# Last projection in 96-column tiles, quartered K tiles in layer 1, one contiguous output DMA: a decode kernel on one core

## The chip, the cores and the metric

The kernel runs on one core of a Trainium2 chip. The metric is the device time of one execution in microseconds (us). Three runs of the kernel before gave 2551.93, 2552.01 and 2552.08 us; their median is 2552.01 us.

## The reference

Two token rows (B = 2, one token each, D = 576 columns) go through two layers. A layer has two blocks, each with its input normalised and added back to the residual x. Cut to what matters:

```python
x = x + A(layernorm(x), k_cache, v_cache, wq, wo)    # 32 heads of 128, 16384 cached positions
x = x + B(layernorm(x), w1, w2, w3, w4)

# A: q = x @ wq; softmax(q . K / sqrt(128)) @ V, per batch row and head; then @ wo
# B: h = gelu(layernorm(x) @ w1), shifted along the sequence, @ w2 -> hs
#    x1 = x + hs
#    return x1 + gelu(layernorm(x1) @ w3) @ w4      # w3: 576x4608, w4: 4608x576
```

The output is x after both layers, 2 x 576 in bf16. The K and V caches are 64 tiles of 4 MiB each (two rows by 32 heads), and both layers read all of them.

## The kernel before, in words

**Layout.** x is held transposed: 128 partitions by KT = 5 column tiles by B = 2. Four tiles cover columns 0 to 511, the fifth covers columns 448 to 575, and only its upper 64 partitions count (`kcol`, `TL` = 64). A projection with few output columns (`rows_step`, line 908 for its matmuls) loads a 128 x 128 block of the weight matrix into TensorE as the stationary operand and streams two columns of activations through it, so that each matmul has two moving columns and one weight load of 128 columns. For w4 these are 36 blocks of K times 5 column tiles, 180 matmuls.

**Memory and queue.** Weights and caches go through one SBUF area, `mem`, with six slots of 32 KiB per partition (`plan_all`, `Store`). Every load is issued by SyncE (line 98) in the order in which `plan_all` queues it. `Store.pump` issues the next load of the queue as soon as the cells it needs have been released, and it waits for the readers of those cells. A whole K or V tile is 128 rows of 32 KiB; a tile planned in `parts` is loaded in that many pieces, each with its own wait.

**Attention.** For each of the 64 (row, head) pairs, half of the scores come from TensorE (transposes at line 1184, evacuation by ScalarE at line 1200, matmuls at 1210) and half from VectorE (`dots`, multiply at line 1240, sum at 1244). `used` releases a whole tile in halves. The pairs run in a loop made by `Graph.loop`.

**Between the layers.** Three K tiles and two V tiles of layer 0 are kept for layer 1. The first K tile of layer 1 is transposed while layer 0 ends: `ahead` issues a group of eight transposes (line 1184), `lay` the ScalarE copy back into the tile (line 699); both do nothing in the tail of layer 1. There are 14 such groups and two more that are held over. They are placed by hand: in `attention`, `last_head`, `two_norms`, the w3 projection, `groups_projection` (w4), `input_norm` and the wq projection of layer 1. In layer 1 `early_scores` (line 1225) reads that tile, and the loads of the first new tiles wait for it and for its followers: V of pair 61 in 4 parts, K of pair 0 whole, K of pair 1 in 2 parts.

**The tail of layer 1.** After the last pair come wo (five loads), `two_norms`, w3 (`cols_projection`, lines 835 and 845), the gelu (lines 995 to 1000), then w4 in eight groups of 6, 6, 6, 6, 6, 3, 2 and 1 blocks (`groups_projection`). Between groups stand a norm on the side (`side_norm`, with a stationary operand in float32, line 711) and the small w1 projection (`h_projection`, line 1337). w1 is loaded by `plan_small`: four full row blocks in one DMA, then the last 64 rows in two DMAs of 56 and 8 rows. Two VectorE additions (`add_rows`, line 596) make `xo`; `finish` transposes its five tiles back on TensorE (line 1316), copies 2 x 576 out of PSUM (line 1319), and SyncE writes the two rows to DRAM.

Of the kernel before, what the change touches and what calls it, by code (L numbers as in the profile page):

```python
# [32 lines left out]
class Graph:  # L33
# [48 lines left out]
        o.deps += [w for w in dict.fromkeys(self.writer[k] for k in reads)]  # L82
        return o

    def dma(self, sem, starts, reads=(), writes=()):

        if sem not in self.dma_sems:
            self.dma_sems[sem] = self.nc.alloc_semaphore(sem)
            self.dma_count[sem] = 0
        o = Op("sync", None)  # L90
        o.sem = sem
        self.dma_count[sem] += 16 * len(starts)
        o.val = self.dma_count[sem]
        h = self.dma_sems[sem]

        def fn(sp):
            for dst, src in starts:
                sp.dma_start(dst, src).then_inc(h, 16)  # L98
            return None
        o.fn = fn  # L100
        return self._add(o, reads, writes)
# [230 lines left out]
class KB:  # L332
    NL = 2
# [13 lines left out]
    PK = ["prod", "gT", "hf", "every", "y0", "y"]  # L347
    GROUPS = (6, 6, 6, 6, 6, 3, 2, 1)
    HEAD = (200, 60)

    def __init__(self, nc, A_x, K, V, wq, wo, w1, w2, w3, w4, out):
        self.nc = nc
# [30 lines left out]
    def _alloc(self):  # L383
        nc = self.nc
        sb = nc.alloc_sbuf_tensor
        B, U, KT, MT, NL = self.B, self.U, self.KT, self.MT, self.NL
        self.size = self.AUX + self.NSLOT * self.TILE
        self.mem = sb("mem", [128, self.size // 2], BF16)
        w = self.CH * 128
# [47 lines left out]
        self.junk = sb("junk", [128, 1], FP32)  # L437
        self.xn2 = sb("xn2", [128, NL, KT, B], BF16)
        self.zero = sb("zero", [128, KT, B], BF16)
        self.xo = sb("xo", [128, KT, B], BF16)  # L440
        self.mv = sb("mv", [128, 3, B], FP32)
        self.hm = sb("hm", [128, 2, B], FP32)
        self.sc = sb("sc", [128, 9, B], FP32)
# [65 lines left out]
    def plan_all(self):  # L509

        B, D = self.B, self.D
        row, w3r, wqr = 2 * D, 2 * self.F, 2 * 128 * self.H
        g = [row * n for n in self.GROUPS]
        self.cuts, self.korder = {}, {}
        s = [self.slot(i) for i in range(self.NSLOT)]
        source = {"k": self.K, "v": self.V}

        tiles = self.tile_order(0)
        place = [(i + 2) % 6 for i in range(len(tiles))]
        place[-1] = 4  # L520
# [14 lines left out]
        b = a + w3r // 2  # L535
        c = b + 4 * g[0]
        e = b + g[6] + g[7]
        self.plan_groups(0, [b, b + g[0], b + 2 * g[0], b + 3 * g[0], 0, g[4], b, b + g[6]])
        assert c <= s[1] and g[4] + g[5] <= b and e <= c
        self.plan_cols("wq", 1, self.wq, [full(1, hd, e), full(2, hd, e + wqr), full(3, hd, e + 2 * wqr),  # L540
                                          full(4, hd, 0), full(0, hd, wqr // 2)])
        assert e + 3 * wqr <= s[1] and wqr // 2 + wqr <= e

        tiles = self.tile_order(1)
        ring = [i if i < 2 else (i + 1) % 6 for i in range(len(tiles))]
        for i, (t, u) in enumerate(tiles):
            self.plan_tile(source[t], t, u, ring[i], (4, 1, 2)[i] if i < 3 else 1, None if i else [1, 2, 3, 0])
        assert ring[-6:] == [4, 5, 0, 1, 2, 3]
        self.plan_heads(1, [s[4], s[4] + r8, s[4] + 2 * r8, s[5], s[4] + 3 * r8])
        a = s[5] + row * self.WO_CUT  # L550
        self.plan_small("w1", 1, self.w1, a, (0, 56, 64))
        a += row * self.KT
        self.plan_cols("w3", 1, self.w3, [full(0, mt, a), full(1, mt, a + w3r), full(2, mt, s[0]), full(3, mt, s[0] + w3r),
                                          full(4, mt, s[0] + 2 * w3r)])
        assert a + 2 * w3r <= self.size
        b = s[0] + 2 * w3r + w3r // 2
        assert b + g[0] <= s[1]
        self.plan_groups(1, [b, s[1], s[1] + g[1], s[1] + g[1] + g[2], s[1] + 3 * g[1], s[1] + 4 * g[1], s[2], s[2] + g[6]])
# [50 lines left out]
    def build(self):  # L609
# [11 lines left out]
                  reads=["ident"], writes=["ident"])  # L621
        for t, k in ((self.x, "x"), (self.st[:, 1, :, :], "st1"), (self.st[:, 2, :, :], "st2"), (self.xb[:, :, :], "xb"),
                     (self.x1[:, :, :], "x1"), (self.hs[:, :, :], "hs"), (self.zero[:, :, :], "zero"),
                     (self.xn[:, :, :], "xn"), (self.xo[:, :, :], "xo"), (self.xn2[:, :, :, :], "xn2"),
                     (self.q_f[:, :], "q_f")):
            self.pool(lambda e, t=t: e.memset(t, 0.0), writes=[k])
        def f(e):
# [31 lines left out]
    def layer(self, l):  # L659
# [6 lines left out]
        self.spread_tail()  # L666
        z = self.sps[0][:, 0:self.MT * self.B]
        self.cols_projection("w3", l, z, ("sps", 0), self.MT)
        self.between_norms()
        self.gelu_z(z)  # L670
        self.groups_projection(l)

# [64 lines left out]
    def input_norm(self, l):  # L737
        self.tt(self.st[:, 1, :, :], self.x, self.x, ALU.mult, ["x"], ["st1"])
        self.stats(2, self.mps, "mps", self.flat(0, 2), ["x", "st1"])
        self.ahead(1 - l, 2)  # L740
        self.scale_of()
        self.touch(ACT.Exp)
        self.lay(1 - l, 2)
# [3 lines left out]
    def two_norms(self, l):  # L747
# [2 lines left out]
        self.tt(self.st[:, 1, :, :], self.x, self.x, ALU.mult, ["x"], ["st1"])  # L750
        self.tt(self.st[:, 2, :, :], self.x, self.hs[:, :, :], ALU.mult, ["x", "hs"], ["st2"])
        self.stats(3, self.mps, "mps", self.flat(0, 3), ["x", "st1", "st2"])
        self.ahead(l, 3)
        m, e2, xc, y0, y = self.mv[:, 0, :], self.mv[:, 1, :], self.kb(self.xc), self.kb(self.y0), self.kb(self.y)
        self.tt(s[:, 0, :], m, m, ALU.mult, ["mv"], ["s0"])
        self.tt(s[:, 5, :], m, hm[:, 0, :], ALU.mult, ["mv", "hm"], ["s5"])
# [10 lines left out]
        self.recip(s[:, 6, :], s[:, 4, :], ["s4"], ["s6"])  # L767
        self.sqrt(s[:, 7, :], s[:, 6, :], ["s6"], ["s7"])
        self.touch(ACT.Sigmoid)
        self.lay(l, 4)  # L770
        self.tt(self.xn[:, :, :], y, self.over_k(s[:, 7, :]), ALU.mult, ["y", "s7"], ["xn"])

    def between_norms(self):

        KT, TL = self.KT, self.TL
        n, y0 = KT - 1, self.kb(self.y0)
# [2 lines left out]
        self.dv(lambda e: e.tensor_copy(out=self.xb[:, 0:n, :], in_=y0[:, 0:n, :]), reads=["y0"], writes=["xb"])  # L779
        self.dv(lambda e: e.tensor_copy(out=self.xb[TL:, n, :], in_=y0[TL:, n, :]), reads=["y0"], writes=["xb"])  # L780
        self.tt(self.x, self.x, self.x1[:, :, :], ALU.add, ["x", "x1"], ["x"])

    def side_norm(self, l):

# [112 lines left out]
                 ["mv", "hm"], ["hm"])  # L897
        self.tt(self.hsc[:, :, :], self.hs[:, :, :], self.over_k(self.hm[:, 0, :]), ALU.subtract, ["hs", "hm"], ["hsc"])

    def rows_step(self, buf, a, b, ps, rhs, rk, pk, nm, first):  # L900

        KT, B, D = self.KT, self.B, self.D

        def f(pe):
            for k in range(a, b):
                for t in range(KT):
                    o = (k - a) * D + self.kcol[t]
                    ins = pe.matmul(ps[:, t * B:(t + 1) * B], lhsT=buf[:, o:o + 128], rhs=rhs(k),
                                    start=first and k == a and t == 0, stop=False, skip_group_check=True)
            return ins  # L910
        self.pe(f, reads=[rk] + self.store.keys(nm), writes=[pk])
# [65 lines left out]
    def groups_projection(self, l):  # L977
        n = len(self.GROUPS)
        for i, (a, b) in enumerate(self.cuts["w4", l]):
            nm = ("w4", l, i)  # L980
            self.rows_step(self.store.buf(nm), a, b, self.mps, lambda k: self.gT[:, k * self.B:(k + 1) * self.B],
                           "gT", "mps", nm, i == 0)
            if i < 3:
                self.ahead(l, 1)
            if i < 4:
                self.lay(l, 1)
            if i == 1:
                self.side_norm(l)
            if i == 2 and l == self.NL - 1:
                self.h_projection()  # L990
        last = l == self.NL - 1
        self.add_rows(self.xo[:, :, :] if last else self.x, "xo" if last else "x", self.mps, "mps")

    def gelu(self, z, zk, a, b, dst, keys):
        self.act(lambda e: e.activation(out=a, in_=z, func=ACT.Square), reads=[zk], writes=keys)
# [86 lines left out]
    def last_head(self, l, s, u):  # L1082
# [11 lines left out]
        self.normed(l, 0, first)  # L1094
        self.ahead(l, 1)
        self.dealt(0, late, self.sps[2], ("sps", 2), self.masked[0], self.oA[:, :], "oA")
        self.ahead(l, 1)
        self.softmax_exp(s)
        self.touch(ACT.Sqrt)
        self.lay(l, 2)  # L1100
# [59 lines left out]
    def used(self, l, t, u, b0, n):  # L1160
# [1 line left out]
        if l == 0 and (t, u) in self.held():  # L1162
            return
        whole = (t, u) in self.store.where
        parts = 2 if whole else self.parts[t, u]
        size = self.NB // parts
        part = b0 // size
        self.uses[t, u, part] = self.uses.get((t, u, part), 0) + n
        if self.uses[t, u, part] == size:
            del self.uses[t, u, part]  # L1170
            if whole:
                self.store.release((t, u), part * self.TILE // 2, (part + 1) * self.TILE // 2)
            else:
                self.store.release((t, u, part))

# [133 lines left out]
    def finish(self):  # L1309
        g, KT, B, D = self.g, self.KT, self.B, self.D  # L1310
        mb = self.mps[:, :].bitcast(BF16)

        def f(pe):
            for t in [KT - 1] + list(range(KT - 1)):
                c = self.kcol[t]
                ins = pe.transpose(mb[0:B, c:c + 128], self.xo[:, t, :], self.ident[:, :])
            return ins
        self.pe(f, reads=["xo", "ident"], writes=["mps"])
        self.dv(lambda e: e.tensor_copy(out=self.rows[0:B, 0:D], in_=mb[0:B, 0:D]), reads=["mps"], writes=["prod"])
        o = g.dma("out", [(self.out.rearrange("b s d -> (b s) d"), self.rows[0:B, 0:D])], reads=["prod"])  # L1320
        g.op("sync", lambda sp: None, reads=["out_done"])
        g.ops["sync"][-1].deps.append(o)

# [66 lines left out]
```

## Time and profile before

| what | value |
|---|---|
| median of three runs | 2552.01 us |
| the profiled execution, its own time | 2552.28 us |
| span of its profile | 2550.6 us |
| read from HBM | 1094.21 MB |
| mean rate over the span | 429 GB/s |
| busy: PE, DVE, ACT, POOL | 60%, 74%, 44%, 6% |

The span runs from the first to the last instruction of the profile; 1.68 us of the profiled execution lie outside it. PE is the row of the matmuls, PEld that of the weight loads, which overlap the matmuls. A line such as L908 is line 908 of the kernel; a helper such as the SyncE issue (L98) has one line for all its calls. In the timeline a row begins with its start and its busy time in us, then engine, line, operation and operands, a count, and in brackets the idle time before it and what ended it.

### The profile page before, as it was taken

The numbers are of one execution on the slowest core, as the hardware profiler recorded it, in microseconds if no ns is written. First come the engines' busy times: TensorE is split into PE (matmuls) and PEld (weight loads), VectorE is DVE, ScalarE is ACT, GpSimd is POOL, SyncE is SP. The second block draws the span as 40 slices with busy tenths as digits, with TensorE's granted clock in tenths as the row PEclk, the third lists the DMA queues.
The fourth block names the chain that finished last, engine by engine and source line by source line (L and its number), as shares of the span: only waits on it lengthen the run. The fifth ranks groups of instructions, "written<-read, shape, count | busy, mean of one in ns | idle before, by whom it ended". The sixth has DMA issues, their size and how long they took to land.

```text
span 2550.6 us, 75213 instructions
## 1 busy us (share of the span) xinstructions
PE 1522.6 (60%) x34456; PEld 1432.9 (56%) x34456; DVE 1888.3 (74%) x1924; ACT 1113.7 (44%) x1831; POOL 162.1 (6%) x151
## 2 busy tenths in 40 slices
PE   4655555655555565556687655655565565556556
PEld 4555555555555555555677655555555455555555
DVE  5877777777777777777649877777777777777773
ACT  3434443443444344444355544443444344344432
POOL 0000000000000000000000000000000000000000
PEclk8666666666666666666667666666666666666665
DMA  9999999999999999999999999999999999999999
GB/s 412 428 434 430 433 431 433 430 433 431 433 431 433 430 433 430 433 430 434 425 417 431 431 434 430 433 430 433 430 433 430 434 430 433 431 433 431 433 431 376
DMA packets 44900, 1094.77 MB, mean 429 GB/s; under 512 B 4922, under 2 KB 6334, under 8 KB 9662
## 3 DMA queue, kind: packets, MB, share of 16 engines
q1 hardware_dynamic: 44862, 1094.23, 100.0%
q8 instruction: 28, 0.46, 0.1%
q14 instruction: 10, 0.08, 0.0%
HBM read 1094.21 MB, written 0.00 MB: 429 GB/s over the span
## 4 chain that ended last, share of the span: by engine, by line
DMA 71%; DVE 19%; issue 8%; PE 1%; SPq 0%; POOLq 0%; DVEq 0%; ACT 0%
DMA mem<-in_A_k_cache_dram 64%; DVE s_dve L1244 9%; DVE prod L1240 9%; DMA mem<-in_A_wo_dram 3%; DMA mem<-in_B_w_dram 2%; DMA mem<-in_A_v_cache_dram 2%; DMA mem<-in_A_wq_dram 0%; DVE mx L1249 0%; PE tps L1184 0%; DVE diag L1138 0%; DVE mx L1257 0%; SPq L98 0%; DVE q_col L1129 0%; DVE o_acc L1281 0%; DVE mx L1255 0%
## 5 line engine op out<-in xcount | busy, mean ns | idle before, releaser
L1200 ACT ACTIVATE mem<-tps 128x1024 bf16<-128x1024 bf16 x1018 | 955.7, 1036 | 1290.0 <-PE tps L1184 1287.5
L1184 PE MATMUL tps<-ident,mem 128*128 128x128 bf16 x8256 | 823.3, 271 | 707.8 <-POOLq L187 707.2
L1244 DVE TENSOR_REDUCE s_dve<-prod 128x16 f32<-128x2048 bf16 x508 | 1161.3, 2286 | 17.4
L1184 PEld LDWEIGHTS tps<-ident,mem 128*128 128x128 bf16 x8256 | 677.6, 124 | 717.7 <-POOLq L187 716.8
L1240 DVE TENSOR_TENSOR prod<-mem,qb 128x2048 bf16<-128x2048 bf16 x508 | 620.6, 1222 | 527.4 <-POOLq L187 518.9
L1300 PE MATMUL mps<-p,mem 128*128 128x1 bf16 x16384 | 450.7, 165 | 85.3 <-POOLq L187 78.2
L1300 PEld LDWEIGHTS mps<-p,mem 128*128 128x128 bf16 x16384 | 443.3, 103 | 100.2 <-ACT p L1274 97.0
L1210 PE MATMUL sps<-q_col,mem 128*128 128x1 bf16 x8144 | 368.7, 167 | 159.2 <-ACT mem L1200 142.9
L1210 PEld LDWEIGHTS sps<-q_col,mem 128*128 128x128 bf16 x8144 | 320.3, 101 | 217.4 <-ACT mem L1200 212.7
L1260 POOL PARTITION_ALL_REDUCE mx<-mx x128 | 160.2, 1252 | 2331.1 <-DVE mx L1257 2331.1
L1270 ACT ACTIVATE p<-s_dve,mx 128x64 bf16<-128x64 f32 x128 | 44.5, 348 | 15.5
L1148 ACT ACTIVATE qb<-sps 128x128 bf16<-128x128 f32 x129 | 34.0, 263 | 33.5 <-PE sps L1145 33.5
L1145 PE MATMUL sps<-diag,ones_bf 128*128 128x128 bf16 x129 | 29.8, 231 | 21.6 <-DVE diag L1138 21.6
L1274 ACT ACTIVATE p<-sps,mx 128x64 bf16<-128x64 f32 x128 | 37.5, 293 | 0.0
L1268 ACT ACTIVATE mx<-mx 128x1 f32<-128x1 f32 x128 | 30.6, 239 | 14.4 <-POOL mx L1260 14.4
L1138 DVE TENSOR_SCALAR diag<-ident,q_f 128x128 bf16<-128x128 bf16 x129 | 31.6, 245 | 0.0
L1249 DVE TENSOR_REDUCE mx<-s_dve 128x1 f32<-128x64 f32 x128 | 28.2, 220 | 4.5
L835 PE MATMUL sps<-xn,mem 128*128 128x2 bf16 x544 | 21.8, 175 | 12.3 <-DMA mem<-in_A_wq_dram 6.2
L835 PEld LDWEIGHTS sps<-xn,mem 128*128 128x128 bf16 x544 | 20.7, 122 | 13.5 <-DMA mem<-in_A_wq_dram 6.8
L1255 DVE TENSOR_REDUCE mx<-sps 128x1 f32<-128x64 f32 x128 | 27.4, 214 | 0.7 <-DVEq L259 0.7
L1145 PEld LDWEIGHTS sps<-diag,ones_bf 128*128 128x128 bf16 x129 | 12.6, 97 | 22.6 <-DVE diag L1138 22.6
L1274 ACT ACTIVATION_READ_ACCUMULATOR p<-sps,mx (+1 forms) x128 | 24.2, 189 | 0.0
(115 smaller groups left out, 225.8 us busy)
## 6 DMA issues: line engine op xcount, KB each, us to landing
mem<-in_A_v_cache_dram SPq DMA_DIRECT2D x125, 4096.0 KB, 45.5
mem<-in_A_k_cache_dram SPq DMA_DIRECT2D x124, 4096.0 KB, 43.1
mem<-in_B_w_dram SPq DMA_DIRECT2D x10, 864.0 KB, 15.0
mem<-in_A_wq_dram SPq DMA_DIRECT2D x8, 1024.0 KB, 12.5
mem<-in_A_wo_dram SPq DMA_DIRECT2D x6, 1152.0 KB, 38.6
mem<-in_B_w_dram SPq DMA_DIRECT2D x6, 1152.0 KB, 16.6
mem<-in_B_w_dram SPq DMA_DIRECT2D x8, 576.0 KB, 9.3
mem<-in_A_v_cache_dram SPq DMA_DIRECT2D x4, 1024.0 KB, 8.7
```

What stands on the lines that cost most here:

```text
L835: ins = pe.matmul(out[:, m * B:(m + 1) * B], lhsT=buf[:, c:c + 127 * d + 1:d], rhs=self.xn[:, k, :], start=first and m == lo, stop=False, ...
L1145: self.pe(lambda pe: pe.matmul(qps, lhsT=self.ones_bf[:, :], rhs=self.diag[:, :], start=True, stop=True, skip_group_check=True), reads=["o ...
L1148: self.act(lambda e: e.activation(out=self.qb[s % self.NS][:, :], in_=qps, func=ACT.Copy), reads=[("qps", i)], writes=[("qb", s % self.NS) ...
L1184: ins = pe.transpose(self.tps[t][:, j * 128:(j + 1) * 128], buf[:, j * 128:(j + 1) * 128], self.ident[:, :])
L1200: self.act(lambda e: e.activation(out=self.kt[k], in_=self.tps[t][:, :].rearrange("p (i c) -> p i c", i=self.CH), func=ACT.Copy), reads=[( ...
L1210: ins = pe.matmul(self.sps[sp][:, c * self.CH + j:c * self.CH + j + 1], lhsT=self.kt[k][:, j, :], rhs=self.q_col[:, sp:sp + 1], start=True ...
L1240: self.dv(lambda e: e.tensor_tensor(out=prod, in0=buf.rearrange("p (j d) -> p j d", d=128), in1=qbc, op=ALU.mult), reads=[("qb", s % self. ...
L1244: self.dv(lambda e: e.tensor_reduce(out=sd[:, c0:c0 + DB], in_=prod, axis=AX.X, op=ALU.add), reads=["prod"], writes=[("s_dve", s % self.NS ...
L1260: self.pool(lambda e: e.partition_all_reduce(self.mx[:, 3, m:m + 1], self.mx[:, 2, m:m + 1], channels=128, reduce_op=ROP.max), reads=[("mx ...
L1270: self.act(lambda e: e.activation(out=p[:, n:self.NB], in_=self.s_dve[s % self.NS][:, :], func=ACT.Exp, bias=self.mx[:, 4, m:m + 1], scale ...
L1274: self.act(lambda e: e.activation(out=p[:, 0:n], in_=self.sps[i][:, 0:n], func=ACT.Exp, bias=self.mx[:, 4, m:m + 1], scale=self.scale, acc ...
L1300: ins = pe.matmul(self.mps[:, 448:449], lhsT=buf[:, j * 128:(j + 1) * 128], rhs=p[:, col:col + 1], start=(h == 0 and b == 0), stop=(h == 1 ...
```

## The change

- **w4 of layer 1** is multiplied in six column tiles of 96 (`EC`) instead of five of 128: 216 matmuls whose stationary operand has 96 columns. Layer 0 keeps 128.
- **x for the addition** is copied to the matching layout by GpSimd: `recut`, at the end of `between_norms` in layer 1, in 13 copies of 32 to 96 partitions into `x6`. The memset of `xo` is gone.
- **The end** has one addition instead of two, one transpose of a 96 x 12 tile instead of five, one copy of 12 x 96, and an output DMA of 12 rows of 192 bytes that are contiguous in DRAM.
- **First K tiles of layer 1**: pair 0 and pair 1 in four parts each, in the order in which their slots come free; V of pair 61 stays in four. Whole tiles are released in quarters instead of halves.
- **w1 of layer 1**: the last 64 rows in eight DMAs of 8 rows.
- **`ahead` and `lay`** are placed differently: `input_norm` 2 to 1, `two_norms` 3 to 2 (`lay` 4 to 3), the second place in `last_head` 1 to 2, one more place in the w4 loop (`lay` in two more).

The diff, cut to its core (the new argument of `dma` is not used by any call):

```diff
+    EC = 96
...
-            self.plan_tile(source[t], t, u, ring[i], (4, 1, 2)[i] if i < 3 else 1, None if i else [1, 2, 3, 0])
+            self.plan_tile(source[t], t, u, ring[i], 4 if i < 3 else 1,
+                           ([1, 2, 3, 0], [1, 3, 0, 2], [0, 2, 1, 3])[i] if i < 3 else None)
...
-        self.plan_small("w1", 1, self.w1, a, (0, 56, 64))
+        self.plan_small("w1", 1, self.w1, a, (0, 8, 16, 24, 32, 40, 48, 56, 64))
...
-        self.ahead(1 - l, 2)
+        self.ahead(1 - l, 1)
...
-        self.ahead(l, 3)
+        self.ahead(l, 2)
...
-        self.lay(l, 4)
+        self.lay(l, 3)
...
+    def recut(self):
+
+        KT, TL = self.KT, self.TL
+        at = [(t, p) for t in range(KT) for p in range(0 if t < KT - 1 else TL, 128, 32)]
+        g = 0
+        while g < len(at):
+            (t, p), (j, q) = at[g], divmod(32 * g, self.EC)
+            n = 1
+            while g + n < len(at) and q + 32 * n < self.EC and at[g + n][0] == t and self.spans(p, n + 1) and self.spans(q, n + 1):
+                n += 1
+            self.pool(lambda e, t=t, p=p, j=j, q=q, n=n: e.tensor_copy(out=self.x6[q:q + 32 * n, j, :],
+                                                                      in_=self.x[p:p + 32 * n, t, :]),
+                      reads=["x"], writes=["x6"])
+            g += n
...
-                for t in range(KT):
-                    o = (k - a) * D + self.kcol[t]
-                    ins = pe.matmul(ps[:, t * B:(t + 1) * B], lhsT=buf[:, o:o + 128], rhs=rhs(k),
+                for t, c in enumerate(cols):
+                    o = (k - a) * D + c
+                    ins = pe.matmul(ps[0:m, t * B:(t + 1) * B], lhsT=buf[:, o:o + m], rhs=rhs(k),
                                     start=first and k == a and t == 0, stop=False, skip_group_check=True)
...
-                           "gT", "mps", nm, i == 0)
-            if i < 3:
+                           "gT", "mps", nm, i == 0, 128 if l < self.NL - 1 else self.EC)
+            if i < 3 or i == 4:
                 self.ahead(l, 1)
-            if i < 4:
+            if i < 6:
                 self.lay(l, 1)
...
+        m = self.EC
+        self.tt(self.xo[0:m, :, :].rearrange("p b t -> p t b"), self.x6[0:m, :, :],
+                self.mps[0:m, 0:self.ET * self.B].rearrange("p (t b) -> p t b", b=self.B), ALU.add,
+                ["x6", "mps"], ["xo"])
...
         self.dealt(0, late, self.sps[2], ("sps", 2), self.masked[0], self.oA[:, :], "oA")
-        self.ahead(l, 1)
+        self.ahead(l, 2)
...
-        parts = 2 if whole else self.parts[t, u]
+        parts = 4 if whole else self.parts[t, u]
...
-        def f(pe):
-            for t in [KT - 1] + list(range(KT - 1)):
-                c = self.kcol[t]
-                ins = pe.transpose(mb[0:B, c:c + 128], self.xo[:, t, :], self.ident[:, :])
-            return ins
-        self.pe(f, reads=["xo", "ident"], writes=["mps"])
-        self.dv(lambda e: e.tensor_copy(out=self.rows[0:B, 0:D], in_=mb[0:B, 0:D]), reads=["mps"], writes=["prod"])
-        o = g.dma("out", [(self.out.rearrange("b s d -> (b s) d"), self.rows[0:B, 0:D])], reads=["prod"])
+        m, n = self.EC, self.ET * B
+        self.pe(lambda pe: pe.transpose(mb[0:n, 0:m], self.xo[0:m, :, :].rearrange("p b t -> p (b t)"),
+                                        self.ident[0:m, 0:m]), reads=["xo", "ident"], writes=["mps"])
+        rows = self.rows[0:n, 0:m]
+        self.dv(lambda e: e.tensor_copy(out=rows, in_=mb[0:n, 0:m]), reads=["mps"], writes=["prod"])
+        o = g.dma("out", [(self.out.rearrange("b s (t c) -> (b s t) c", c=m), rows)], reads=["prod"])
```

More of the change, by code (lines that the diff above doesn't have):

```diff
@@ L83, in relay, with dma @@
         return o
-    def dma(self, sem, starts, reads=(), writes=()):
+    def dma(self, sem, starts, reads=(), writes=(), eng="sync"):
         if sem not in self.dma_sems:
@@ L89, in dma @@
             self.dma_count[sem] = 0
-        o = Op("sync", None)
+        o = Op(eng, None)
         o.sem = sem
@@ L385, in _alloc @@
         sb = nc.alloc_sbuf_tensor
-        B, U, KT, MT, NL = self.B, self.U, self.KT, self.MT, self.NL
+        B, U, KT, MT, NL, D = self.B, self.U, self.KT, self.MT, self.NL, self.D
         self.size = self.AUX + self.NSLOT * self.TILE
@@ L439, in _alloc @@
         self.zero = sb("zero", [128, KT, B], BF16)
-        self.xo = sb("xo", [128, KT, B], BF16)
+        self.ET = D // self.EC
+        self.x6 = sb("x6", [128, self.ET, B], FP32)
+        self.xo = sb("xo", [128, B, self.ET], BF16)
         self.mv = sb("mv", [128, 3, B], FP32)
@@ L623, in build @@
                      (self.x1[:, :, :], "x1"), (self.hs[:, :, :], "hs"), (self.zero[:, :, :], "zero"),
-                     (self.xn[:, :, :], "xn"), (self.xo[:, :, :], "xo"), (self.xn2[:, :, :, :], "xn2"),
+                     (self.xn[:, :, :], "xn"), (self.xn2[:, :, :, :], "xn2"),
                      (self.q_f[:, :], "q_f")):
@@ L668, in layer @@
         self.cols_projection("w3", l, z, ("sps", 0), self.MT)
-        self.between_norms()
+        self.between_norms(l)
         self.gelu_z(z)
@@ L769, in two_norms, with between_norms @@
         self.touch(ACT.Sigmoid)
-        self.lay(l, 4)
+        self.lay(l, 3)
         self.tt(self.xn[:, :, :], y, self.over_k(s[:, 7, :]), ALU.mult, ["y", "s7"], ["xn"])
-    def between_norms(self):
+    def between_norms(self, l):
         KT, TL = self.KT, self.TL
@@ L781, in between_norms, with spans @@
         self.tt(self.x, self.x, self.x1[:, :, :], ALU.add, ["x", "x1"], ["x"])
+        if l == self.NL - 1:
+            self.recut()
+    def recut(self):
[11 more added lines that the diff above has]
+            g += n
+    @staticmethod
+    def spans(p, n):
+        return p == 0 or p % 64 == 0 and n <= 2 or n == 1
     def side_norm(self, l):
@@ L898, in hs_projection, with rows_step @@
         self.tt(self.hsc[:, :, :], self.hs[:, :, :], self.over_k(self.hm[:, 0, :]), ALU.subtract, ["hs", "hm"], ["hsc"])
-    def rows_step(self, buf, a, b, ps, rhs, rk, pk, nm, first):
-        KT, B, D = self.KT, self.B, self.D
+    def rows_step(self, buf, a, b, ps, rhs, rk, pk, nm, first, m=128):
+        B, D = self.B, self.D
+        cols = self.kcol if m == 128 else range(0, D, m)
         def f(pe):
             for k in range(a, b):
-                for t in range(KT):
-                    o = (k - a) * D + self.kcol[t]
-                    ins = pe.matmul(ps[:, t * B:(t + 1) * B], lhsT=buf[:, o:o + 128], rhs=rhs(k),
+                for t, c in enumerate(cols):
+                    o = (k - a) * D + c
+                    ins = pe.matmul(ps[0:m, t * B:(t + 1) * B], lhsT=buf[:, o:o + m], rhs=rhs(k),
                                     start=first and k == a and t == 0, stop=False, skip_group_check=True)
@@ L990, in groups_projection @@
                 self.h_projection()
-        last = l == self.NL - 1
-        self.add_rows(self.xo[:, :, :] if last else self.x, "xo" if last else "x", self.mps, "mps")
+        if l < self.NL - 1:
+            self.add_rows(self.x, "x", self.mps, "mps")
+            return
+        m = self.EC
+        self.tt(self.xo[0:m, :, :].rearrange("p b t -> p t b"), self.x6[0:m, :, :],
+                self.mps[0:m, 0:self.ET * self.B].rearrange("p (t b) -> p t b", b=self.B), ALU.add,
+                ["x6", "mps"], ["xo"])
     def gelu(self, z, zk, a, b, dst, keys):
@@ L1171, in used @@
             if whole:
-                self.store.release((t, u), part * self.TILE // 2, (part + 1) * self.TILE // 2)
+                self.store.release((t, u), part * self.TILE // 4, (part + 1) * self.TILE // 4)
             else:
```

## The prediction

> **What bounds the kernel now.** I read the page first: its slices, then the chain that ended last.
>
> ```profile
> span 2550.6 us, 75213 instructions
> PEclk8666666666666666666667666666666666666665
> DMA  9999999999999999999999999999999999999999
> GB/s 412 428 434 430 433 431 433 430 433 431 433 431 433 430 433 430 433 430 434 425 417 431 431 434 430 433 430 433 430 433 430 434 430 433 431 433 431 433 431 376
> DMA 71%; DVE 19%; issue 8%; PE 1%; SPq 0%; POOLq 0%; DVEq 0%; ACT 0%
> ```
>
> The DMA engines are busy in every slice, and the rate sits at 430 to 434 GB/s except at the start, around the middle (425, 417) and in the last slice (376). The chain is DMA for 71%. So the bytes set the time, 1.09 GB are read before and after, and an edit can win only where the rate dips, or lose where work stands behind the last bytes. Next I read the timeline of the end, TensorE's weight loads alone, then everything behind them, and the same microseconds by windows.
>
> ```profile
> 2536.85 0.88 PEld L908 LDWEIGHTS mps<-prod,mem 128*128 128x128 bf16 x30 [1.46 <-DVE prod L1000]
> 2538.38 0.88 PEld L908 LDWEIGHTS mps<-prod,mem 128*128 128x128 bf16 x30 [0.65 <-DMA mem<-in_B_w_dram]
> 2539.18 0.50 PEld L711 LDWEIGHTS sps<-st,mean_f 128*128 128x128 f32 x2
> 2540.71 0.88 PEld L908 LDWEIGHTS mps<-prod,mem 128*128 128x128 bf16 x30 [1.03 <-DMA mem<-in_B_w_dram]
> 2541.51 0.83 PEld L1337 LDWEIGHTS sps<-xn,mem 128*128 128x128 bf16 x25
> 2542.82 0.88 PEld L908 LDWEIGHTS mps<-prod,mem 128*128 128x128 bf16 x30 [0.48 <-DMA mem<-in_B_w_dram]
> 2544.92 0.88 PEld L908 LDWEIGHTS mps<-prod,mem 128*128 128x128 bf16 x30 [1.22 <-DMA mem<-in_B_w_dram]
> 2546.69 0.58 PEld L908 LDWEIGHTS mps<-prod,mem 128*128 128x128 bf16 x15 [0.25 <-DMA mem<-in_B_w_dram]
> ```
> ```profile
> 2547.39 0.36 DVE L596 TENSOR_TENSOR xo<-st,mps 128x8 bf16<-128x8 f32 x2 [3.00 <-PE mps L908]
> 2547.80 0.69 PE L1316 MATMUL mps<-ident,xo 128*2 128x128 bf16 x5 [0.45 <-DVE xo L596]
> 2548.54 0.45 DVE L1319 COPY prod<-mps 2x576 bf16<-2x576 bf16 x1 [0.79 <-PE mps L1316]
> 2549.01 0.27 SPq L98 DMA_DIRECT2D out_dram<-prod  x1
> ```
> ```profile
> 2542.00:2544.00 2.00, 1.40 (x43) 1.21 (x40) 0.35 (x2) 1.50 (x3) 0.00 (x0) 0.50 0.84 335
> 2544.00:2546.00 2.00, 0.99 (x31) 0.92 (x32) 0.18 (x1) 0.19 (x1) 0.00 (x0) 0.50 0.37 139
> ```
>
> Each w4 group waits for its DMA (0.4 to 1.2 us in the brackets): TensorE finishes a group of 30 loads in 0.88 us and the groups arrive about 2.1 us apart (2540.71, 2542.82, 2544.92). TensorE has room here, a factor of two and a bit. The rate fades to 335 and 139 GB/s before the last bytes land: no cached data is left to move, so whatever is added to TensorE from here on has nothing to hide behind once its room is used up. The granted clock in these rows is 0.50.
>
> **The change part by part.** Start from the profiled execution's own 2552.28 us.
>
> *The 96-column matmuls.* Of 180 matmuls 216 remain to be done, each with its own weight load; the two moving columns are the same, so the load sets the spacing. What does a load of 96 columns cost? No row shows one. Three tiny windows, each on the first load after an idle engine or in a stream, show other shapes, and one stream of float32 loads.
>
> ```profile
> L908 PEld LDWEIGHTS mps<-prod,mem 128*128 128x128 bf16 x1 | 0.1, 105 | 0.2 <-DMA mem<-in_B_w_dram 0.2
> L1316 PEld LDWEIGHTS mps<-ident,xo 128*2 128x2 bf16 x1 | 0.1, 79 | 0.5 <-DVE xo L596 0.5
> L711 PEld LDWEIGHTS sps<-st,mean_f 128*128 128x128 f32 x1 | 0.3, 290 | 0.0
> 2510.98 0.93 PEld L932 LDWEIGHTS sps<-l,mean_f 128*128 128x128 f32 x4
> ```
>
> Thirty bf16 loads of 128 columns take 0.88 us: one of 105 ns and 29 more, so (880 - 105) / 29 = 26.7 ns apart, or 0.21 ns a column. Two columns take 79 ns, which I take for the fixed part. Then 105 - 79 = 26 ns is what 128 bf16 columns add, the spacing again. A float32 load takes 290 ns, and four of them 0.93 us, so (930 - 290) / 3 = 213 ns apart: 1.67 ns a column, eight times as slow. The transposes of row L1316 stream 128 moving columns each in about (0.69 - 0.27) / 4 = 0.105 us, 0.83 ns a column: that is the array's ordinary step at this clock. So float32 loads go at two steps a column, and the full bf16 load at four columns a step. The four-at-a-time rate is seen on full 128-column bf16 loads alone. The ends for 96 columns: 96 x 0.21 = 20 ns, and at the float32 rate 96 x 1.67 = 160 ns. I take one column a step, 96 x 0.83 = **80 ns**, the ordinary step of the array between the two ends; that the fourfold rate is lost is the choice on which this forecast stands.
>
> The Trainium skill's page "TensorE: Matmul & The Clock Gate", section "Weight-path perf modes", says that fast weight load is switched on only when the number of weights is 128 and the type isn't float32, in four chunks of 32 columns. By it and by the page's formula in "LDWEIGHTS (loading the stationary operand)", columns over 1.2 GHz, a 96-column load is estimated at 80 ns, the same sum; with the fast mode kept at 96 columns the sum would be that of rival 1. The trace agrees on what it shows, 26.7 ns against 213 ns; nothing in it shows 96.
>
> Now the stage, from 2536.85, when the gelu releases the first group. Six blocks are 36 loads, 36 x 0.080 = 2.88 us against arrivals 2.1 us apart, so TensorE no longer waits for DMA and the loads simply add up: 216 x 0.080 = 17.28, the norm's float32 loads 0.50, w1's loads 0.83, together 18.61 us. The stream ends at 2555.46. Before, it ended at 2546.69 + 0.58 = 2547.27 with the last load's 0.105 inside; its start spacing ended at about 2547.19. Difference **+8.27 us**, all of it in the open. The side norm on VectorE and ScalarE is done long before w1's turn at 2545.99 (it took until 2541.51 with the loads starting at 2539.18, 2.3 us; here they start at 2542.61).
>
> *The end.* One addition of 12 columns for two: 0.36 to 0.18, -0.18. One transpose for five: the first result takes about 0.27 of the 0.69, and it streams 96 columns, -0.43. The copy has 96 elements a row for 576: 0.45 to about 0.20, -0.25 (bounds 0 and -0.35). The output is 2.3 KB either way, 12 pieces for 2: 0, with 0.1 us either way. Sum **-0.85 us**, all on the path.
>
> *GpSimd's copies.* They wait for x, which is final at 2523.46.
>
> ```profile
> 2523.11 0.35 DVE L596 TENSOR_TENSOR x<-prod,hs 128x8 f32<-128x8 f32 x2
> L1260 POOL PARTITION_ALL_REDUCE mx<-mx x128 | 160.2, 1252 | 2331.1 <-DVE mx L1257 2331.1
> L626 POOL MEMSET xb<- 128x10 f32 x1 | 0.1, 97 | 0.0
> ```
>
> Thirteen copies at 97 to 1252 ns are 1.3 to 16.3 us, done between 2524.8 and 2539.8; the addition comes at 2547 even in the old order. GpSimd has nothing queued behind them. They cost nothing; without that cover, at most the 16.3 us. The dropped memset of `xo` is one such 97 ns row in the prologue: nothing.
>
> *K in quarters, release in quarters, `ahead` and `lay`.* All this is in the middle, where the rate shows what there is to win.
>
> ```profile
> 1300.00:1310.00 10.00, 7.37 (x147) 6.86 (x147) 1.53 (x10) 3.51 (x5) 0.00 (x0) 0.50 1.01 422
> 1310.00:1350.00 40.00, 34.31 (x795) 32.22 (x795) 34.63 (x41) 26.03 (x39) 2.83 (x3) 0.72 1.01 420
> 1360.00:1400.00 40.00, 28.50 (x666) 26.41 (x664) 38.60 (x41) 24.27 (x41) 3.76 (x3) 0.75 1.00 432
> 1291.82 1.01 PE L1184 MATMUL tps<-ident,mem 128*128 128x128 bf16 x8
> ```
>
> Over the 40 us in which the first new tiles arrive the rate is 420 against 432 later: (432 - 420) / 432 x 40 = 1.1 us is all that earlier issues can return. Against it, two 4.19 MB tiles in 8 KiB rows could go at the 422 GB/s of the stretch where V's quarters start: 8.39 MB x (1/422 - 1/432) = +0.46 us. SyncE gets eight waits for three; behind each stands the next quarter or tile, and the quarters are listed in the order in which the slots are read free. The transposes that move are one group out of the input norm, 1.01 us of TensorE, into the w4 loop of layer 0, where TensorE waits for DMA as it does in layer 1's rows above; the others move among places of layer 0's tail. Taken together between -1.1 and +0.5; I take **-0.3 us**.
>
> *w1 in eight pieces.*
>
> ```profile
> L98 SPq DMA_DIRECT2D mem<-in_B_w_dram x16: 294/1513/29253, 2473.0 to 2528.1; - x16
> mem<-in_B_w_dram SPq DMA_DIRECT2D x4, 1152.0 KB, 17.6
> ```
>
> Six issues more at 0.29 to 1.5 us are 1.8 to 9 us of SyncE ahead of every w3 and w4 load. A w3 load takes 17.6 us from issue to landing, of which its own 1152 KB need 2.7 us at 433 GB/s, so about 15 us of cover. How the last 72 KB spread over the engines moves the landing by no more than their own transfer, 0.17 us either way. I take 0; without cover it would be the 9 us.
>
> **Sum**: 2552.28 + 8.27 - 0.85 - 0.3 = 2559.4 in the profiled execution's terms. That execution lies 0.27 us above the median of the runs, so **2559.1 us** is forecast, +0.28%.
>
> **The rivals.**
>
> 1. *96-column loads keep the fast rate.* Place: the spacing of line 908's loads in the last 10 us. At 27 ns a group takes 36 x 0.027 = 1.0 us and still waits for DMA; nothing is added, the gains stay: 2552.01 - 0.85 - 0.3 = 2550.9 us, not slower. It decides by the spacing s: the stage holds 216 s + 1.33 us against 10.34 us now, so with the gains of 1.15 us the change breaks even at s = 47 ns and is slower by over 5.1 us from about 71 ns. For it: the bf16 rows. Against: every load seen that isn't 128 bf16 columns lacks that rate.
> 2. *The clock rises.* TensorE becomes busy without a gap for 18 us. If the granted clock went to 1.0 after some 5 us, the rest would go at 40 ns: 62 loads at 80, 154 at 40 and w1 and the norm halved, 11.9 us for 10.34, +1.5: 2552.4 us. Against it stands the end of the last pair, where loads with one moving column fill TensorE and the clock stays at 0.50 then and after.
>
> ```profile
> 2507.60:2511.00 3.40, 3.40 (x128) 3.40 (x129) 0.28 (x1) 0.05 (x1) 0.00 (x0) 0.50 1.02 428
> 2511.00:2549.00 38.00, 22.74 (x561) 20.87 (x558) 7.29 (x47) 5.56 (x11) 0.00 (x0) 0.50 0.89 362
> ```
>
> The Trainium skill's same page, section "What's actually happening", has the clock gate open after one busy window of about 3.4 us. By that rule rival 2 would come true; the rows above, 3.40 us full at 0.50, say that such loads do not count as busy.
>
> 3. *96 columns at the float32 rate.* 160 ns: 216 x 0.160 + 1.33 = 35.9 us, +25.5: 2576.4 us. For it: the only slow stream that the trace shows; against: float32 is twice as wide.
>
> **How the numbers follow.** Forecast 0.70, rival 1 0.13, rival 2 0.06, rival 3 and spacings between 0.07, and 0.04 for a slip of the middle, half of it to either side. The forecast's own range is 2557.8 to 2560.8: the middle's ends -0.8 and +0.8 about the value taken, w1's 0.17, the end's 0.2, and 4 ns of spacing, 0.9 us upwards. With rivals 1 and 2 the range goes from 2550.4 to 2561.0 and leaves about 0.11 outside. A change of 0.2% (5.1 us) is about what a measurement of this kernel can tell from none: faster by over it 0.02, within it rivals 1 and 2 and a little, 0.21, slower 0.77.
>
> **What would show it.** In the profile after: 216 loads of 128x96 at line 908, near 80 ns apart, with no DMA wait before the later groups; the end of that stream near 2555.5; clock 0.50; one transpose and one addition behind it, under 1 us together with the copy; the middle's rate over 420. The forecast is wrong if the groups still wait for DMA.

## The result, and the profile after

The changed kernel takes 2560.89 us (median of 7 runs, 2559.99 to 2561.05) against 2552.01 us (7 runs, 2551.73 to 2552.99): ratio 1.0034, interval 1.0024 to 1.0044. It is slower by 8.9 us; 7.1 us were forecast. The profiled execution took 2560.89 us, 8.61 us more than that of before.

The tail of layer 1 carries the answer. The weight loads of TensorE in the changed kernel, in order of time (start, busy time, count, and in brackets the idle time before):

```profile
2537.93 5.83 PEld L934 LDWEIGHTS mps<-prod,mem 128*96 128x96 bf16 x72 [1.46 <-DVE prod L1031]
2543.65 0.54 PEld L715 LDWEIGHTS sps<-st,mean_f 128*128 128x128 f32 x2
2544.07 3.00 PEld L934 LDWEIGHTS mps<-prod,mem 128*96 128x96 bf16 x36
2546.94 0.89 PEld L1366 LDWEIGHTS sps<-xn,mem 128*128 128x128 bf16 x25
2547.84 8.71 PEld L934 LDWEIGHTS mps<-prod,mem 128*96 128x96 bf16 x108
```

Line 934 is the old line 908. No group waits for DMA any more: the only bracket is the gelu's, ahead of the first load. The group of 36 takes 3.00 us, its last load's own 195 ns included: (3.00 - 0.195) / 35 = 0.080 us apart. The last 108 are as far apart: (8.71 - 0.195) / 107 = 0.080 us. In the same stretch the loads by shape (count, busy us, mean ns of one), and two windows of it, in which the DMA rate fades while TensorE is full. A window row gives its length, busy time and count of PE, PEld, DVE, ACT and POOL, then the granted clock of TensorE (1 is full speed), the busy share of the DMA engines and GB/s:

```profile
L934 PEld LDWEIGHTS mps<-prod,mem 128*96 128x96 bf16 x216 | 17.5, 195 | 1.5 <-DVE prod L1031 1.5
```
```profile
2542.00:2544.00 2.00, 2.00 (x26) 2.00 (x25) 0.00 (x0) 0.00 (x0) 0.00 (x0) 0.50 0.72 289
2544.00:2546.00 2.00, 2.00 (x26) 2.00 (x26) 0.90 (x6) 0.20 (x1) 0.00 (x0) 0.50 0.34 133
```

Behind the loads stands the short end, one addition, one transpose, one copy and the output:

```profile
2556.75 0.19 DVE L600 TENSOR_TENSOR xo<-x,mps 96x12 bf16<-96x12 f32 x1 [6.87 <-PE mps L934]
2556.99 0.24 PE L1345 MATMUL mps<-ident,xo 96*12 96x96 bf16 x1 [0.35 <-DVE xo L600]
2557.28 0.20 DVE L1348 COPY prod<-mps 12x96 bf16<-12x96 bf16 x1 [0.34 <-PE mps L1345]
2557.50 0.34 SPq L98 DMA_DIRECT2D out_dram<-prod  x1
```

The span is 2559.2 us now, 2550.6 before. The 8.61 us fall into three parts. From the first w4 load to the addition: 2537.93 to 2556.75, 18.82 us, against 2536.85 to 2547.39, 10.54 us: **+8.28**. From the addition to the end of the span: 2.45 against 3.21 us: **-0.76**. And w4 starts later, 2537.93 for 2536.85: **+1.08**.

The middle, in the window from 1310 to 1350 us in which the new tiles arrive:

```profile
1310.00:1350.00 40.00, 34.70 (x791) 33.56 (x792) 34.58 (x41) 26.07 (x39) 2.79 (x3) 0.66 1.02 423
```

The rate there is 423 GB/s for 420, a little higher as hoped, and yet w4 starts 1.08 us later. (Over all runs below, the same window has 423 to 426 GB/s in the six kernels with the quarters and 417 to 426 in the seven without: a single 420 against 423 is within the scatter.) GpSimd's 13 copies took 3.07 us from 2524.35 and were long done:

```profile
2524.35 3.07 POOL L799 COPY x<-st 96x2 f32<-96x2 f32 x13 [19.11 <-DVE st L600]
```

Two questions are left for experiments: whether the 8.28 us are really the lost load rate, and whose the 1.08 us are.

### The profile page after: what moved, and what is told of

Read it like the earlier page. It is cut to its first block, busy times and chain, and to the rows that moved or that the text cites. A ratio compares the mean times of both kernels' runs of the same rounds, so it can differ in the third digit from the quotient of the medians.

```text
span 2559.2 us, 75300 instructions
## 1 busy us (share of the span) xinstructions
PE 1536.0 (60%) x34488; PEld 1450.5 (57%) x34488; DVE 1887.9 (74%) x1923; ACT 1115.5 (44%) x1831; POOL 164.5 (6%) x163
## 4 chain that ended last, share of the span: by engine, by line
DMA 70%; DVE 19%; issue 8%; PE 2%; SPq 0%; POOLq 0%; DVEq 0%; ACT 0%
DMA mem<-in_A_k_cache_dram 63%; DVE s_dve L1275 9%; DVE prod L1271 9%; DMA mem<-in_A_v_cache_dram 3%; DMA mem<-in_B_w_dram 2%; DMA mem<-in_A_wo_dram 1%; PE mps L934 1%; DMA mem<-in_A_wq_dram 0%; DVE mx L1280 0%; DVE diag L1169 0%; DVE mx L1288 0%; DVE q_col L1160 0%; DVE o_acc L1312 0%; DVE mx L1286 0%; SPq L98 0%
## 5 line engine op out<-in xcount | busy, mean ns | idle before, releaser
L934 PE MATMUL mps<-prod,mem 128*96 128x2 bf16 (+1 forms) x396 | 23.5, 194 | 3.4 <-DVE prod L1031 1.9
```

The lines of the kernel that those rows point to most:

```text
L934: ins = pe.matmul(ps[0:m, t * B:(t + 1) * B], lhsT=buf[:, o:o + m], rhs=rhs(k), start=first and k == a and t == 0, stop=False, skip_group_ ...
```

## The experiments

Medians in us, with the kernel before on the same chip; the interval is that of the ratio. "w4 starts" is the first load of layer 1's w4 in the profiled execution.

| kernel | median (range) | before | ratio, interval | w4 starts |
|---|---|---|---|---|
| e1, 96-column part alone | 2559.86 (2559.67 to 2560.97) | 2552.26 | 1.0030 (1.0019 to 1.0042) | 2536.93 |
| e2, w1 in two pieces | 2560.42 (2559.97 to 2560.54) | 2552.26 | 1.0031 (1.0019 to 1.0043) | 2537.58 |
| e3, loads 128 wide | 2552.52 (2551.77 to 2553.61) | 2552.26 | 1.0001 (0.9992 to 1.0010) | 2537.75 |
| e4, without the 96-column part | 2552.67 (2552.18 to 2553.86) | 2552.26 | 1.0002 (0.9993 to 1.0011) | 2537.93 |
| f1, wide loads, short end, nothing else | 2551.63 (2551.39 to 2552.03) | 2552.29 | 0.9998 (0.9989 to 1.0007) | 2536.82 |
| f2, w1 in eight pieces alone | 2552.55 (2551.92 to 2553.32) | 2552.29 | 1.0001 (0.9992 to 1.0010) | 2537.68 |
| f3, quarters and moved transposes alone | 2552.69 (2552.26 to 2553.18) | 2552.29 | 1.0001 (0.9992 to 1.0010) | 2537.28 |
| f4, tiles of 64 columns | 2560.82 (2560.42 to 2560.94) | 2552.29 | 1.0033 (1.0019 to 1.0048) | 2537.49 |
| g1, f1 with one narrow tile of six | 2552.03 (2551.49 to 2552.29) | 2552.29 | 0.9999 (0.9990 to 1.0008) | 2536.83 |
| g2, f1 with three narrow tiles of six | 2554.50 (2554.04 to 2555.73) | 2552.29 | 1.0010 (1.0001 to 1.0019) | 2537.29 |
| g3, f1 with w1 in one piece | 2552.09 (2551.58 to 2552.47) | 2552.29 | 0.9999 (0.9990 to 1.0008) | 2536.86 |

**e1_only_96**: the changed kernel with everything but the 96-column part put back:

```diff
-        self.plan_small("w1", 1, self.w1, a, (0, 8, 16, 24, 32, 40, 48, 56, 64))
+        self.plan_small("w1", 1, self.w1, a, (0, 56, 64))
-            self.plan_tile(source[t], t, u, ring[i], 4 if i < 3 else 1,
-                           ([1, 2, 3, 0], [1, 3, 0, 2], [0, 2, 1, 3])[i] if i < 3 else None)
+            self.plan_tile(source[t], t, u, ring[i], (4, 1, 2)[i] if i < 3 else 1, None if i else [1, 2, 3, 0])
...
```

> The kernel before with the 96-column part alone (tiles, copies by GpSimd, one addition, one transpose, contiguous output); K tiles, w1 and the places of the transposes as before. Theory L (a 96-column load takes 80 ns because it loses the fast rate; the 1.1 us later start of w4 seen in the changed kernel belongs to w1's eight pieces): w4 starts near 2536.9 as before, its loads are 80 ns apart, about 2552.0 + 8.3 - 0.8 = 2559.5 us. Rival M (the later start comes with the 96-column part itself, for example from GpSimd's copies): start near 2537.9 and 2560.6 us or more.

2559.86 us, 7.6 us above before, and w4 starts at 2536.93, as before. The 96-column part carries the slowdown and does not make the start later; its first 72 loads take 5.83 us, as in the changed kernel. Rival M falls.

**e3_wide_loads**: the same six tiles, wide loads:

```diff
+                    n = m if k == b - 1 and c + 128 > D else 128
-                    ins = pe.matmul(ps[0:m, t * B:(t + 1) * B], lhsT=buf[:, o:o + m], rhs=rhs(k),
+                    ins = pe.matmul(ps[0:n, t * B:(t + 1) * B], lhsT=buf[:, o:o + n], rhs=rhs(k),
```

> The changed kernel, but TensorE loads 128 columns for each of the six tiles (the 32 columns beyond a tile only fill partitions that nothing reads), except for the last tile of a group's last block, where there is nothing behind; still 216 matmuls, 96-column layout, one addition, one transpose. Theory L: 208 loads go at 27 ns and 8 at 80, a group of six blocks takes about 1.0 us, w4 waits for its DMA again, the +8.3 us are gone: about 2552.6 us. Rival S (the cost is that of 216 matmuls instead of 180, or of the new layout): stays near 2560.9 us.

2552.52 us. Still 216 matmuls, still the new layout, and 8.4 us are gone. Its first three w4 groups in order of time:

```profile
2537.75 1.09 PEld L935 LDWEIGHTS mps<-prod,mem 128*128 128x128 bf16 x36 [1.46 <-DVE prod L1032]
2539.29 1.09 PEld L935 LDWEIGHTS mps<-prod,mem 128*128 128x128 bf16 x36 [0.45 <-DMA mem<-in_B_w_dram]
2541.41 1.09 PEld L935 LDWEIGHTS mps<-prod,mem 128*128 128x128 bf16 x36 [0.60 <-DMA mem<-in_B_w_dram]
```

Thirty-six loads take 1.09 us instead of 3.00, and the waits for DMA are back in the brackets. A load that brings 32 unused columns is three times as fast as one that leaves them out. Rival S falls.

**f4_tiles_64**:

```diff
-    EC = 96
+    EC = 64
-        self.x6 = sb("x6", [128, self.ET, B], FP32)
+        self.x6 = self.l1[:, 0:self.ET * B].rearrange("p (t b) -> p t b", b=B)
```

> The changed kernel with nine tiles of 64 columns in place of six of 96 (324 matmuls, the copies by GpSimd into the buffer of l1, which is free by then, output in 18 rows of 128 bytes). Theory C (a load costs 0.83 ns a column at this clock, whatever its width below 128): 53 ns apart, 324 x 0.0533 = 17.3 us as with 96, about 2561 us. Rival F (a load below 128 columns costs a fixed 80 ns): 324 x 0.080 = 25.9 us, about 2569.5 us.

2560.82 us, as the changed kernel, with 324 loads where that has 216:

```profile
2543.88 2.96 PEld L934 LDWEIGHTS mps<-prod,mem 128*64 128x64 bf16 x54
```
```profile
L934 PEld LDWEIGHTS mps<-prod,mem 128*64 128x64 bf16 x324 | 17.5, 157 | 1.5 <-DVE prod L1031 1.5
```

The first row is the third group in the timeline, the second the loads of the stretch by shape: (2.96 - 0.157) / 53 = 0.053 us apart, and in all the same 17.5 us of busy time as 216 loads of 96. So the price is by the column, 0.83 ns, not by the load; theory C holds, F falls. In all these runs a load and its matmul have the same width, so what is priced is the pair; that the load is the dear half was not tried apart.

**g1_one_narrow** and **g2_three_narrow** test where the price begins to count; both are f1 with some tiles narrow (g1 shown, g2 has `m < 128 and t >= 3`):

```diff
-                    n = m if k == b - 1 and c + 128 > D else 128
+                    n = m if c + 128 > D else 128
```

> f1_wide_only with the sixth tile of every block loaded with 96 columns: 36 loads at 80 ns, 180 at 27 ns. Theory R (a load's price counts only past the room that the DMA leaves): a group of six blocks is 30 x 0.027 + 6 x 0.080 = 1.3 us against arrivals 2.1 us apart, so it is hidden: 2551.7 us, as f1 (2551.63). Rival P (each narrow load costs its share of the 8.3 us): 36/216 of it, +1.4: 2553.0 us.

> f1_wide_only with three of the six tiles loaded with 96 columns: 108 loads at 80 ns, 108 at 27 ns, 53 ns on average, a little past the break-even of the prediction (47 ns). Theory R: a group takes 18 x 0.107 = 1.92 us, with the norm's and w1's 1.3 us between them TensorE falls behind late and ends near 2549.7 instead of 2547.2: +2.5, about 2554.1 us. Rival P: 108/216 of 8.3, +4.1: 2555.8 us.

g1: 2552.03 us, 0.4 above f1; g2: 2554.50 us, 2.9 above f1. Theory R forecast 2551.7 and 2554.1, the share-by-share rival P 2553.0 and 2555.8. Both are nearer to R, each 0.3 to 0.4 us above it. In g1 this need not be the loads: its last w4 landing is also 0.39 us later than f1's (2547.12 for 2546.73). Five of g2's eleven runs lie at 2555.26 to 2555.73 us, close to P, but their spans (2552.2 to 2552.8 us) are no longer than those of the six others (2552.3 to 2552.8): what these five add lies outside the span. The two profiles show the boundary, g1 first: its groups of 36 take 1.36 us and wait, those of g2 run through.

```profile
2538.38 1.36 PEld L934 LDWEIGHTS mps<-prod,mem 128*128 128x128 bf16 x36 [0.20 <-DMA mem<-in_B_w_dram]
2540.81 1.35 PEld L934 LDWEIGHTS mps<-prod,mem 128*128 128x128 bf16 x36 [0.65 <-DMA mem<-in_B_w_dram]
```
```profile
2541.37 2.19 PEld L934 LDWEIGHTS mps<-prod,mem 128*128 128x128 bf16 x36
2544.33 5.83 PEld L934 LDWEIGHTS mps<-prod,mem 128*128 128x128 bf16 x108
2550.36 0.19 DVE L599 TENSOR_TENSOR xo<-x,mps 96x12 bf16<-96x12 f32 x1 [4.00 <-PE mps L934]
```

(The shape of a row is that of its first load; g2's groups are half 96 wide.) g2's addition stands at 2550.36 where f1's stands at 2547.28.

**The later start.** Four kernels divide the rest of the change.

**e2_w1_two**, the changed kernel with `(0, 56, 64)` for w1:

> The changed kernel with w1's last 64 rows again in two DMAs of 56 and 8 rows. Theory W (the eight pieces of 8 rows load some DMA engines more than others, and the slowest of them then delivers w3 about 1 us later): the distance between the first and the last engine's landing of w3 shrinks from 5.5 to about 3.7 us, w4 starts about 1 us earlier, about 2559.8 us. Rival Q (the middle of the kernel, K in quarters, made the start later): no difference, 2560.9 us.

2560.42 us, 0.5 below the changed kernel, not 1.1, and w4 still starts at 2537.58, 0.35 earlier and not 1. The distance between the first and the last landing of w3's first load shrinks from 5.48 to 4.66 us, not to 3.7. Theory W as put there explains half at most.

**e4_no_96**, the changed kernel with the old `rows_step`, `add_rows` and `finish`:

> The changed kernel without the 96-column part (five tiles of 128, two additions, five transposes, output in two rows): what is left of the change is K in quarters, release in quarters, w1 in eight pieces and the moved transposes. Theory W: the last bytes land about 1 us later, 2552.9 us. Rival Q' (the quarters return time in the middle and w1 costs nothing): 2551.4 us. If all of this is neutral: 2552.0 us.

2552.67 us, the median 0.4 above before, its runs from 2552.18 to 2553.86; w4 starts at 2537.93, exactly as in the changed kernel. So the later start belongs to what is left here. The time is nearer to theory W than to no change, though the interval (0.9993 to 1.0011) holds both; rival Q' falls.

**f2_w1_only**, before with w1 in eight pieces, and **f3_quarters_only**, before with K in quarters, release in quarters and the moved transposes:

> The kernel before with w1's last 64 rows in eight DMAs of 8 rows and nothing else changed. Theory W (the pieces delay the slowest DMA engine): w3 lands up to 1 us later, 2552.7 to 2553.3 us. Rival V (the quarters of K and V and the moved transposes make the later start): 2552.3 us, no difference.

> The kernel before with K in quarters, release in quarters and the moved transposes; w1 in two pieces, 128-column tiles. Theory W: the middle is neutral or returns a little, 2551.8 to 2552.3 us. Rival V: the first engine's landing comes earlier by up to 1 us, the last engine's does not, so that the distance between them grows by 1 us and the end is later, 2552.6 to 2553 us.

2552.55 and 2552.69 us, +0.26 and +0.40 by the medians, both inside the intervals: neither alone can be told from no change by its ratio. f2 lies between W and V; f3 lies where V put it, above W's range, so theory W, which blamed w1 alone, does not hold. The starts of w4 tell more, since every kernel has one. They come 2.71 to 2.75 us after the last landing of w3 in all thirteen profiles (2534.12 and 2536.85 in before, 2535.21 and 2537.93 in the changed kernel), so it is w3's last DMA engine that sets them. Sorted by the two parts:

| start of w4 | K, release and transposes as before | K and release in quarters, transposes moved |
|---|---|---|
| w1's last rows in one or two DMAs | 2536.82 to 2537.29, mean 2536.93 (before, e1, f1, g1, g2, g3) | 2537.28 and 2537.58 (f3, e2) |
| w1's last rows in eight DMAs | 2537.68 (f2) | 2537.49 to 2537.93, mean 2537.78 (changed kernel, e3, e4, f4) |

Each part alone goes with a start 0.5 to 0.75 us later, both together with 0.85. These are single executions: g2, which has neither part, starts at 2537.29, as late as f3. In time the two parts together cost 0.4 us by the medians with the old end (e4 against before), 0.9 with the wide loads (e3 against f1) and 1.0 with the narrow ones (the changed kernel against e1); the last two compare kernels of different sets, in which the kernel before differs by 0.03 and 0.25 us.

What the traces show of the way: a DMA's semaphore counts the 16 engines as each finishes, so the landing events give the first and the last of them. Of w4's last load they are 2543.08 and 2547.01 in before, 2542.42 and 2547.86 in the changed kernel, 2542.26 and 2547.25 in f3, 2543.09 and 2547.61 in f2. Over all thirteen, the first engine ends at 2542.13 to 2542.74 with the quarters and at 2542.72 to 2543.68 without them; the last one ends at 2547.61 to 2547.88 with w1 in eight pieces and at 2546.73 to 2547.51 otherwise. So the quarters bring the first engine forward and not the last, and w1's pieces go with a last landing about half a microsecond later. The pieces also show in the rate just behind them, from 2516 to 2522: 375 to 384 GB/s in the five kernels with eight, 393 to 401 in the eight others, at the same busy share of the engines (1.05 to 1.06). The engines were on average as busy as before, and moved less.

Why the last engine gains nothing from the quarters, and by what way small pieces slow the rate, was not tried.

**f1_wide_only** and **g3_w1_whole**: the short end without the rest, then with w1's last rows in one DMA, `(0, 64)`.

> The kernel before with the 96-column layout and its short end, but TensorE loading 128 columns for all but the last tile of a group's last block, as in e3; K tiles, w1 and the places of the transposes as before. Theory: the loads are hidden behind the DMA again and the end is 0.8 us shorter: 2552.26 - 0.8 = 2551.4 us. Rival (the last DMA landing or the output's 12 pieces eat the shorter end): 2552.2 us.

> f1_wide_only with w1's last 64 rows in one DMA, 4 rows on each of 16 engines, in place of 56 and 8 rows. Theory W (what w1's split puts on the DMA engine that lands last moves the end): at most 0.2 us either way, 2551.4 to 2551.8 us, and a distance between the first and the last landing of w4 that differs from f1's 3.05 us by some tenths. Rival (each further DMA of w1 costs time by itself): one DMA less, 0.05 us or less, nothing to see.

f1: 2551.63 us, 0.66 below before, near the forecast of 2551.4. It is the fastest kernel of all, though its interval (0.9989 to 1.0007) holds no change as well. g3: 2552.09 us, above f1 by 0.5, more than the 0.2 that either side allowed. Its first and last landing of w4 lie 4.12 us apart, a whole microsecond more than f1's and not some tenths, and the last one is 0.48 us later (2547.21 for 2546.73). But this distance goes from 3.05 to 4.52 us among the six kernels that have neither part, so one profile can't carry theory W; what moved g3 stays open.

## Why the prediction was right, point by point

- **The total**: 2559.1 us were forecast and 2560.89 measured, 0.09 us above the forecast's own range (2557.8 to 2560.8) and inside the one that the rivals widen to 2561.0.
- **The 96-column loads**: +8.27 us were forecast and +8.28 measured, at 80 ns a load as chosen. e3 shows the cause (128 columns on the same six tiles: gone) and f4 the step (0.83 ns a column at 96 and at 64). The Trainium skill's page "TensorE: Matmul & The Clock Gate", section "Weight-path perf modes", ties the fast rate to exactly 128 weights that aren't float32; the trace now agrees at 96 and 64 columns, 80 and 53 ns for 27.
- **The room of TensorE**: right. With the waits for DMA gone the loads add up; g1 and g2 put the break between 36 and 108 narrow loads, as the sum with 47 ns had it.
- **The end**: -0.85 forecast, -0.76 measured; the copy and the transpose came out at 0.20 and 0.24 us for 0.20 and 0.26 taken. The output in 12 pieces was set at 0; from its issue to its last landing it took 1.27 us for 1.16, and that is the rest.
- **GpSimd's copies**: hidden, 3.07 us in a cover that reached to 2556.
- **The middle and w1**: -0.3 and 0 were forecast, +1.08 measured in the profiled execution, and this is nearly the whole miss: 1.38 of 1.49 us between the sum of 2559.4 and the execution's 2560.89. The step that failed is the one that turned a rate into time: "(432 - 420) / 432 x 40 = 1.1 us is all that earlier issues can return". A mean over 16 engines says nothing of the engine that lands last, and w4 starts 2.7 us after that one has landed: the last landing of w3 came at 2535.21 for 2534.12. For w1 the bound of 0.17 us took the mean as well, while f2, with the pieces alone, starts w4 0.75 us later than the mean of the kernels without either part. The forecast of SyncE's cover fits: its eight pieces put the first w3 issue at 2512.2 for 2508.6, and the first engine's landing of that load came no later, 2519.89 for 2520.53 and 2520.63 in f2; the last engine's did, 2525.37 and 2524.66 for 2524.20.
- **Rival 1** (the fast rate stays) is refuted by the rows, **rival 3** (float32 rate) by the 80 ns. **Rival 2** (the clock rises) is refuted too: the granted clock stays at 0.50 through 18 us of full TensorE (the row below, a window of the changed kernel: weight loads busy 17.97 of 18 us, then the clock). The same page, section "What's actually happening", has the gate open after one busy window of about 3.4 us; here loads with two moving columns fill TensorE five times as long at 0.50, so by that rule they did not count as busy. The prediction's sum for this rival is a slip: 62 x 0.080 + 154 x 0.040 + 0.67 is 11.8 us, not 11.9, and moves its time by 0.1 us.

```profile
2538.00:2556.00 18.00, 18.00 (x237) 17.97 (x238) 1.46 (x10) 2.81 (x5) 0.00 (x0) 0.50 0.36 144
```

## What to carry to other kernels

Where the moving side has only a few columns, the weight load sets the price of a matmul. Of the bf16 widths tried here, 64, 96 and 128 columns, the load of 128 is the cheapest: keep loads 128 wide even if some columns are thrown away, and let the surplus land in output partitions that nothing reads. TensorE work beside the last loads costs time only past the room that their arrivals leave, so work out that break-even spacing before changing a tile's shape. At the end of a stream of loads ask which DMA engine lands last, not what the mean rate is.

## What the runs showed of the hardware that was not expected

- At granted clock 0.50 a bf16 load of 128 columns takes 26.7 ns of the stream, one of 96 takes 80 and one of 64 takes 53: the narrower load is two to three times as dear.
- A load of 128 bf16 columns does not always go at 26.7 ns either. In before, w3's 36 loads of a block take 1.64 us, (1.64 - 0.14) / 35 = 43 ns apart on average; in 30 of them the columns lie six elements apart in the buffer (`block_cols`), in w4's they are neighbours.
- TensorE full of loads for 18 us did not raise the granted clock from 0.50.
- SyncE's issue of one small w1 piece took up to 28.8 us in the changed kernel (8 rows) and 29.3 us before (56 rows). Whether that delays a landing was not tried.

```profile
L98 SPq DMA_DIRECT2D mem<-in_B_w_dram x22: 306/654/28762, 2473.1 to 2529.9; - x22
```

- The 16 DMA engines end w4's last load 3.9 us apart in before and 5.4 us apart in the changed kernel (the landing events above); without the quarters and w1's pieces it is 3.05 to 4.52 us, from one execution to the next.
